# One transfer for the tail rows of the Q and K weights, all gate and up loads on one queue, and new orders for five engines

## The chip, the cores and the metric

The kernel runs on one core of a Trainium2 chip. The metric is the time of one execution in device microseconds; a profiled execution also gives the span, from the first to the last instruction of the program. Five engines work side by side: TensorE (PE in the profile; its weight loads are PEld), VectorE (DVE), ScalarE (ACT), GpSimd (POOL) and SyncE (SP). SP only issues transfers here. ACT issues some, between its activations.

## The reference

The computation is one transformer block on 2048 tokens of width 448: layer norm, linear attention with 16 heads of 28, a residual, a second layer norm, a gated Gelu MLP of width 1792, and a residual.

```python
def _A_ref(x, wqkv, wo):                      # x: layer norm of the input
    qkv = (x @ wqkv) ...                      # split into q, k, v by head
    phi = lambda t: jnp.where(t > 0, t + 1, jnp.exp(t)) + 1e-6
    pq, pk = phi(q), phi(k)
    kv = jnp.einsum("bhsd,bhse->bhde", pk, v)
    z = jnp.einsum("bhsd->bhd", pk)
    num = jnp.einsum("bhqd,bhde->bhqe", pq, kv)
    den = jnp.einsum("bhqd,bhd->bhq", pq, z)[..., None] + 1e-6
    return (num / den) ... @ wo

def _B_ref(x, w_gate, w_up, w_down):
    return (gelu(x @ w_gate) * (x @ w_up)) @ w_down

h = x + _A_ref(_layernorm(x), wqkv, wo)
h2 = h + _B_ref(_layernorm(h), w_gate, w_up, w_down)
```

Inputs and outputs are bf16; sums are kept in fp32.

## The kernel before

**Tiles.** The 2048 tokens are 16 tiles of 128. The width 448 is taken as three blocks of 128 rows and a tail of 64, so the weights of Q, K and V lie in four blocks of partitions; the fourth holds 64 rows of weights and 64 rows of zeros.

**First stage, per tile t.** DVE takes the statistics of the row (`bnst1_t`, L414, and `bnag1_t`, L415). ACT makes the inverse deviation with a logarithm and an exponential (`ln1_t`, `rstd1_t`, L421 and L423). Tiles 0 to 3 are normalized by DVE (`normD_t`, L436), transposed by PE (`tr0_t`, `tr1_t`, L444) and copied out in two halves, by ACT (`evxA_t`, L449) and DVE (`evxD_t`, L451). Tiles 4 to 15 are normalized by POOL (`negm1_t`, L418, `normP_t`, L454) and transposed by a transfer on SP's queue (`xT_t`, L456). Then PE projects (L470): step `k_t` or `q_t`, four matmuls of 448 columns, one for each block of rows, the fourth with the tail rows. ACT takes the exponential of K (`ek_t`, L481), DVE clips and adds (`ck_t`, L482, `pk_t`, L483), and PE sums the products of pk with the normalized rows over all tiles (`pt4_t`, from tile 10 on `pt1_t` and `pt3_t`, L489). For Q, ACT makes `eq_t` and `rq_t` (L497, L498). The projections take turns on four banks of PSUM, so each waits until the one four places earlier (in the order in which the program makes them) has been read.

**Middle.** The sums become, with the V weights, the key-value matrices (`kv`, L528), and with the output weights the matrices `w2` (L548). Two copies by transfer (`dws0`, `dws1`, written to `pt_sb`) swap the halves of `w2`. The denominators and scaled queries are made in pairs of tiles p (`cqP_p`, L583, `aqP_p`, L584, POOL's `t1p_t`, L586, `drP_p`, L587, ACT's `deP_p`, L589, `rdP_p`, L590, `pnP_p`, L591). They are transposed by a transfer (`oT_p`, L606), and PE makes the attention output in two steps (`outA_p`, `outB_p`, L628 and L629). DVE adds the residual (`hr_t`, L634) and takes the statistics of the second layer norm; POOL makes its power and negated mean (`vpe2`, `pow2`, `negm2`, L426, L427, L418) and normalizes (`nhP_t`, L663), DVE repeats the row once (`wrap_t`, L665), and SP's queue transposes (`hT_t`, L666).

**Last stage.** The MLP works on chunks of 2, 2, 4, 4 and 4 tiles. A step `gu2_v` or `gu4_v` (L727 gate, L729 up) is a set of matmuls with 64 rows: the gate weights and their rows lie on partitions 0 to 63, the up weights on 64 to 127, and a gate and an up matmul run side by side. In 14 steps of the first two chunks (7 each) and 14 of each later chunk the hidden width is covered. ACT takes the Gelu in two halves (`ge0_v`, `ge1_v`, L747), DVE multiplies with the up part (`hm0_v`, `hm1_v`, L749). The gate results take turns on two banks, the up results on two others, so step v needs the products of step v - 2. The down projection is done for pairs of tiles in two parts (`downA_p`, `downB_p`, L697), DVE adds the residual (`fo448_t`, L703), and SP stores the tile (`do_t`, L704; L683 and L684 for the last two tiles).

**What sets the order.** The program records 866 tasks, each with its engine and the buffers that it reads and writes; semaphores follow from these. The order on each engine is written out by hand as a list of task numbers (`ORDERS`), one list for each engine, and nothing moves at run time: an engine that waits for one task holds all tasks behind it in its list. `HOLD` only says which of several waits of a task is placed first. A transfer is issued by the engine whose list it is in, and each of SP and ACT has one queue of transfers; SP's is q1 in the profile, ACT's q10.

**Loads.** x comes in pieces on both queues. `dw0` and `dw1` are the first 384 rows of the K and Q weights, `dw0_t` and `dw1_t` their last 64 rows (the tails), all in `wqk_sb`: K's columns in the second half, Q's in the first. `dwg0` and `dwg1` are the gate weights (first 768 columns, then the rest), `dwu0` and `dwu1` the up weights. Every transfer of these is recorded by one helper, so that all have the line L347.

The loads around the change, before:

```python
dma_w1("act", wqk_sb, D, 2 * D, b_wk, "dw0_t")
tx1 = dma_w1("act", wqk_sb, 0, D, b_wq, "dw1_t")
...
dma("sp", wgu_sb[A_, :, cs], B_w_gate[:, cs]..., [b_wg[i]], "dwg%d" % i, after=xts[-1:])
dma("act", wgu_sb[B_, :, cs], B_w_up[:, cs]..., [b_wu[i]], "dwu%d" % i, after=eks[13:14])
```

Of the kernel before, what the change touches and what calls it, by code (L numbers as in the profile page):

```python
# [12 lines left out]


ORDERS = (
# [34 lines left out]
)  # L50
HOLD = {
# [3 lines left out]
}  # L55


# [173 lines left out]
def bass_sequential_preLN__linear_attn_block__glu_gated_geglu__prompt_kernel(  # L231
    nc, A_x, A_wqkv, A_wo, B_x, B_w_gate, B_w_up, B_w_down, out
):
    S, D, FF, H, DH = 2048, 448, 1792, 16, 28
# [16 lines left out]
    with es:  # L251
# [8 lines left out]
        wqk_sb = sb("wqk_sb", [128, 4, 2 * D], BF16)  # L260
# [45 lines left out]
        def bufs(name, n):  # L306
            return [_Buf("%s%d" % (name, i)) for i in range(n)]
# [4 lines left out]
        b_ones2 = _Buf("ones2")  # L312
        b_wq, b_wk, b_wv = bufs("wq", 2), bufs("wk", 2), bufs("wv", 2)
        b_wpad = bufs("wpad", 2)
        b_wo, b_wg, b_wu, b_wd = _Buf("wo"), bufs("wg", 2), bufs("wu", 2), _Buf("wd")
        b_ident, b_ones, b_mones, b_mtmp, b_mask, b_eps, b_mhalf, b_powtmp = (
            _Buf(n) for n in ("ident", "ones", "mones", "mtmp", "mask", "eps", "mhalf", "powtmp"))
# [28 lines left out]
        def dma(q, out_ap, in_ap, w, name, r=(), after=()):  # L346
            t_ = G.add(q, lambda e: e.dma_start(out_ap, in_ap), r=r, w=w, name=name, kind="dma", after=list(after) + last[q])  # L347
            last[q] = [t_]
            return t_
# [7 lines left out]
        def dma_w1(q, dst, c0, c1, b, name):  # L357
            return dma(q, dst[A_, 3, c0 % (2 * D):c0 % (2 * D) + c1 - c0], A_wqkv[384:448, c0:c1], [b[1]], name)
# [8 lines left out]
        dma_x("act", 1, 2)  # L367
        dma_x("sp", 2, 4)
        dma_w3("act", wqk_sb, D, 2 * D, b_wk, "dw0")
        dma_w1("act", wqk_sb, D, 2 * D, b_wk, "dw0_t")  # L370
        tx1 = dma_w1("act", wqk_sb, 0, D, b_wq, "dw1_t")
        dma_w3("sp", wqk_sb, 0, D, b_wq, "dw1")
        dma_x("sp", 4, 8)
        dma_x("sp", 8, 12)
# [84 lines left out]
        eks = []  # L459
# [11 lines left out]
            return ins  # L471

        def proj_reads(t, b):
            return [(b_xnT[t][0], 0), (b_xnT[t][1], 2), (b[0], 0), (b[1], 3), (b_wpad[0], 3)]

        def k_tile(t):
            bk = slot()
# [31 lines left out]
        for i in range(2):  # L509
            cs = slice(0, FC) if i == 0 else slice(FC, FF)  # L510
            dma("sp", wgu_sb[A_, :, cs], B_w_gate[:, cs].rearrange("(k p) n -> p k n", p=64), [b_wg[i]], "dwg%d" % i, after=xts[-1:])
            dma("act", wgu_sb[B_, :, cs], B_w_up[:, cs].rearrange("(k p) n -> p k n", p=64), [b_wu[i]], "dwu%d" % i, after=eks[13:14])


        op("act", lambda e: e.activation(zbc[B_, :], ps[B_, BK_PT[3], 0:D], AF.Identity), [b_ps[BK_PT[3]]], [b_z[1]], "z1")
# [303 lines left out]
```

## Time and profile before

| | us |
|---|---|
| median of 3 runs | 191.06 |
| lowest and highest | 191.03 and 191.11 |
| the profiled execution, its own time | 191.73 |
| its span, first to last instruction | 190.0 |
| PE busy in it | 184.9 |
| DVE busy | 127.8 |
| ACT busy | 76.6 |
| POOL busy | 51.6 |

The granted TensorE clock is 1.00 throughout. The profile stretches the execution a little: its own time is 0.67 us over the median. In a timeline row the first number is the start in us from the span's start, the second the duration of the row (a row can hold several equal instructions, "x8"), and what stands in brackets is the idle time before it and what ended that. The ends of matmuls are modelled, so two steps of PE are best compared from start to start. In the table of transfers the last number is the time from issue to landing. In the chain of waits each row names what the work that ended last was waiting for.

### The profile page before, as it was taken

How to read it: one execution, taken by the hardware profiler on the slowest of the kernel's cores; microseconds unless marked ns; L12 is line 12 of the kernel's file. 1: busy time of each engine (PE TensorE's matmuls, PEld its weight loads, DVE VectorE, ACT ScalarE, POOL GpSimd, SP SyncE). 2: the span in 40 equal slices, each digit the busy share in tenths (PEclk: the TensorE clock that was granted, in tenths of full speed). 3: DMA queues.
4: the chain of work that ended last, by engine and by line, in shares of the span. 5: the costliest groups of instructions: out<-in, count | busy, mean ns of one | idle time of the engine just before them, and what ended most of it. 6: DMA issues, size and time to landing. Idle time of an engine off the chain costs nothing.

```text
span 190.0 us, 4461 instructions
## 1 busy us (share of the span) xinstructions
PE 184.9 (97%) x1813; PEld 114.9 (60%) x1813; DVE 127.8 (67%) x328; ACT 76.6 (40%) x220; POOL 51.6 (27%) x91
## 2 busy tenths in 40 slices
PE   7899999999999999989999999999999999999994
PEld 7554555555689898855666666555544555555643
DVE  3998869999999995868976933592474234335232
ACT  3688843699963221334331421222244122224100
POOL 6066740514416569003484000019000000000000
PEclk9999999999999999999999999999999999999999
DMA  6995448999394432940020691000590000200004
GB/s 175 373 229 88 86 92 176 210 217 198 70 314 90 85 52 48 105 95 28 0 52 0 117 136 40 0 5 0 121 146 4 3 0 0 76 0 0 3 15 155
DMA packets 35076, 17.11 MB, mean 90 GB/s; under 512 B 26864, under 2 KB 33648, under 8 KB 35056
## 3 DMA queue, kind: packets, MB, share of 16 engines
q1 hardware_dynamic: 33424, 14.65, 37.6%
q10 hardware_dynamic: 1632, 2.18, 5.2%
q8 instruction: 14, 0.23, 0.5%
q14 instruction: 6, 0.05, 0.1%
HBM read 8.26 MB, written 1.84 MB: 53 GB/s over the span
## 4 chain that ended last, share of the span: by engine, by line
PE 78%; DVE 9%; DMA 8%; POOL 2%; SPq 1%; issue 1%; ACT 0%
PE ps L729 29%; PE ps L697 16%; PE ps L470 10%; PE ps L727 9%; PE ps L489 5%; DMA x_sb<-in_A_x_dram 3%; PE ps L679 3%; DMA hnT<-hn 2%; DMA xnT<-xnn 2%; PE ps L628 2%; DVE st L414 2%; POOL hn L663 2%; DVE hh L749 2%; PE ps L629 1%; DVE x_sb L634 1%; DVE pqn L591 1%
## 5 line engine op out<-in xcount | busy, mean ns | idle before, releaser
L727 PE MATMUL ps<-hnT,wgu_sb 64*128 64x512 bf16 (+1 forms) x490 | 89.0, 333 | 0.6 <-DMA hnT<-hn 0.6
L729 PE MATMUL ps<-hnT,wgu_sb 64*128 64x512 bf16 (+1 forms) x490 | 89.0, 333 | 0.0
L747 ACT ACTIVATE gl<-ps 128x256 bf16<-128x256 f32 x112 | 36.8, 381 | 85.0 <-PE ps L727 84.8
L749 DVE TENSOR_TENSOR hh<-ps,gl 128x256 bf16<-128x256 f32 x112 | 42.5, 415 | 36.3 <-ACT gl L747 35.7
L729 PEld LDWEIGHTS ps<-hnT,wgu_sb 64*128 64x128 bf16 x490 | 45.0, 94 | 26.5 <-DVE hh L749 3.0
L727 PEld LDWEIGHTS ps<-hnT,wgu_sb 64*128 64x128 bf16 x490 | 45.2, 94 | 6.0 <-ACT gl L747 0.8
L697 PE MATMUL ps<-wd_sb,hh 64*128 64x448 bf16 x392 | 41.5, 349 | 0.0
L697 PEld LDWEIGHTS ps<-wd_sb,hh 64*128 64x128 bf16 x392 | 24.3, 94 | 13.3 <-issue 0.2
L470 PE MATMUL ps<-wqk_sb,xnT 128*128 128x448 bf16 x128 | 27.3, 353 | 0.7 <-DMA wqk_sb<-in_A_wqkv_dram 0.6
L414 DVE BATCH_NORM_STATS2 st<-x_sb 128x6 f32<-128x448 bf16 x32 | 19.3, 613 | 2.2 <-DMA x_sb<-in_A_x_dram 2.2
L586 POOL TENSOR_TENSOR t<-pq,zbc 128x448 f32<-128x448 bf16 x12 | 13.0, 1104 | 28.4 <-DVE pq L584 28.4
L470 PEld LDWEIGHTS ps<-wqk_sb,xnT 128*128 128x128 bf16 x128 | 12.2, 98 | 12.1 <-DMA wqk_sb<-in_A_wqkv_dram 1.2
L703 DVE TENSOR_TENSOR x_sb<-ps,x_sb 128x448 bf16<-128x448 f32 x14 | 8.6, 617 | 8.9 <-PE ps L697 8.9
L489 PE MATMUL ps<-pk,xnn 128*128 128x448 bf16 x64 | 14.1, 352 | 0.0
L628 PE MATMUL ps<-w,pqnT 64*128 64x448 bf16 x49 | 11.5, 349 | 0.1
L426 POOL TENSOR_SCALAR ln<-mv 128x2 f32<-128x2 f32 x7 | 2.3, 330 | 32.3 <-DVE mv L415 32.0
L481 ACT ACTIVATE e<-ps 128x448 bf16<-128x448 f32 x16 | 8.7, 541 | 6.0 <-PE ps L470 6.0
L663 POOL TENSOR_SCALAR hn<-x_sb,nm,rs 128x448 bf16<-128x448 bf16 x14 | 10.6, 765 | 0.1
L629 PE MATMUL ps<-pt_sb,pqnT 64*128 64x448 bf16 x42 | 10.2, 349 | 0.0
L489 PEld LDWEIGHTS ps<-pk,xnn 128*128 128x128 bf16 x64 | 6.2, 98 | 6.0 <-DVE pk L483 0.8
L634 DVE TENSOR_TENSOR x_sb<-ps,x_sb 128x448 bf16<-128x448 f32 x16 | 9.6, 612 | 0.3 <-PE ps L629 0.3
L483 DVE SCALAR_TENSOR_TENSOR pk<-ps,e 128x448 bf16<-128x448 f32 x16 | 9.6, 611 | 0.1
(83 smaller groups left out, 159.2 us busy)
## 6 DMA issues: line engine op xcount, KB each, us to landing
out_dram<-x_sb SPq DMA_DIRECT2D x15, 112.0 KB, 1.8
wd_sb<-in_B_w_down_dram SPq DMA_DIRECT2D x1, 1568.0 KB, 7.6
x_sb<-in_A_x_dram SPq DMA_DIRECT2D x3, 448.0 KB, 6.6
wgu_sb<-in_B_w_gate_dram SPq DMA_DIRECT2D x1, 896.0 KB, 9.6
wgu_sb<-in_B_w_up_dram ACTq DMA_DIRECT2D x1, 896.0 KB, 12.8
wgu_sb<-in_B_w_gate_dram SPq DMA_DIRECT2D x1, 672.0 KB, 5.9
wgu_sb<-in_B_w_up_dram ACTq DMA_DIRECT2D x1, 672.0 KB, 10.4
wo_sb<-in_A_wo_dram SPq DMA_DIRECT2D x1, 392.0 KB, 8.1
```

The costliest lines, as they stand in the source:

```text
L414: op("dve", lambda e: e.bn_stats(st[:, t, :], src_ap), [b_src], [b_st[t]], "bnst%s_%d" % (tag, t))
L470: ins = e.matmul(ps[:, bk, 0:D], xnT[:, t, k, :], wqk_sb[:, k, c0:c0 + D], start=(k == 0), stop=(k == 3))
L489: ins = e.matmul(ps[:, BK_PT[c], 0:D], xnn[:, t % XN_R, c * 128:(c + 1) * 128], pk[:, ip, :], start=(t == 0), stop=(t == T - 1))
L586: op("pool", lambda e, n=n: e.tensor_tensor(t1[:, n, :], pq[:, a + n, :], zbc[:, :], ALU.mult), [b_pq[a + n]] + b_z, [b_t1[n]], "t1p_%d" % ...
L628: e.matmul(ps[:, BK_OUT[0], 0:D], pqnT[ra, i2, sg // 2, :], w2[ra, sg // 2, :], start=(sg == 0), stop=(sg == 5))
L629: ins = e.matmul(ps[:, BK_OUT[1], 0:D], pqnT[rb, i2, 3 + (sg + 1) // 2, :], (w2 if sg == 6 else w2s)[rb, sg // 2, :], start=(sg == 0), sto ...
L663: op("pool", lambda e, t=t, sh=sh: e.tensor_scalar(hn[:, sh, 0:D], x_sb[:, t, :], nm2[:, t:t + 1], rs2[:, t:t + 1], ALU.add, ALU.mult), [b ...
L697: ins = e.matmul(ps[:, BK_O[n], 0:D], hh[rows, j, sl[n]], wd_sb[rows, j, :], start=(half == 0 and j == 0), stop=(half == 1 and j == NJ - 1))
L727: first = e.matmul(psG[:, jj * N:(jj + 1) * N], wgu_sb[A_, k, j * 128:(j + 1) * 128], hnT[A_, ka_, c0:c0 + N], start=(k == 0), stop=(k == ...
L729: ins = e.matmul(psU[:, jj * N:(jj + 1) * N], wgu_sb[B_, k, j * 128:(j + 1) * 128], hnT[B_, kb_, c0:c0 + N], start=(k == 0), stop=(k == NK ...
L747: G.add("act", lambda e, gi=gi, cs_=cs_, psG=psG: e.activation(gl[:, gi, cs_], psG[:, cs_], AF.Gelu_apprx_tanh), r=[b_ps[BK_G[i]]], w=[b_g ...
L749: op("dve", lambda e, dst=dst, srcU=srcU, srcL=srcL: e.tensor_tensor(dst, srcU, srcL, ALU.mult), [b_ps[BK_U[i]], b_glh], [b_ar[j_][t % HR] ...
```

## The change

Three things are changed at once.

1. The two transfers of the last 64 rows, `dw0_t` (K) and `dw1_t` (Q), become one transfer `dw0_t` of 64 rows by 896 columns on ACT's queue. All projections, K and Q, now wait for the one buffer `b_wt` before their fourth matmul. There are 865 tasks instead of 866.
2. The up loads `dwu0` and `dwu1` move from ACT's list to SP's. SP issues `dwg0 dwu0 dwg1 dwu1` in a row behind the last transpose of x, and the swap copies `dws0 dws1` and the transpose `oT_1` follow.
3. The lists of all five engines are new (every number in them also shifts by one), and so is `HOLD`.

```diff
-        dma_w1("act", wqk_sb, D, 2 * D, b_wk, "dw0_t")
-        tx1 = dma_w1("act", wqk_sb, 0, D, b_wq, "dw1_t")
+        tx1 = dma("act", wqk_sb[A_, 3, :], A_wqkv[384:448, 0:2 * D], [b_wt], "dw0_t")
...
-            return [(b_xnT[t][0], 0), (b_xnT[t][1], 2), (b[0], 0), (b[1], 3), (b_wpad[0], 3)]
+            return [(b_xnT[t][0], 0), (b_xnT[t][1], 2), (b[0], 0), (b_wt, 3), (b_wpad[0], 3)]
...
-            dma("act", wgu_sb[B_, :, cs], B_w_up[:, cs].rearrange("(k p) n -> p k n", p=64), [b_wu[i]], "dwu%d" % i, after=eks[13:14])
+            dma("sp", wgu_sb[B_, :, cs], B_w_up[:, cs].rearrange("(k p) n -> p k n", p=64), [b_wu[i]], "dwu%d" % i, after=xts[-1:])
```

The lists, by the names of the tasks, where the prediction speaks of them ("-" before, "+" after):

```diff
 PE, start
-tr0_0 tr1_0 tr1_1 tr0_1 k_0 q_0 tr1_2 tr0_2 tr0_3 tr1_3 k_1 k_2 k_3 pt4_0 pt4_1 q_1 q_2 pt4_2 k_4 q_3 pt4_3 k_5
+tr0_0 tr1_0 tr0_1 tr1_1 k_0 tr0_2 tr1_2 k_1 q_0 tr0_3 tr1_3 k_2 k_3 pt4_0 q_1 pt4_1 pt4_2 q_2 k_4 pt4_3 k_5 q_3
 PE, middle
-pt3_13 q_4 pt3_14 pt3_15 q_5 q_6 kv q_7 q_10 w2_2 w2_1 w2_3 w2_0 tro_1 q_9 tro_0 q_8 out1_1 out1_0 q_11 q_12 q_13 q_15 q_14 trh_1
+pt3_13 pt3_14 pt3_15 q_5 q_4 kv q_7 q_8 w2_2 w2_0 w2_1 q_9 w2_3 tro_1 tro_0 q_6 out1_1 out1_0 q_10 q_11 q_13 q_12 q_14 q_15 trh_1
 PE, first two chunks of the MLP
-outA_3 gu2_6 outB_3 downA_0 gu2_7 gu2_8 downB_0 gu2_9 outA_4 gu2_10 outB_4 gu2_11 gu2_12 gu2_13 gu4_14 gu4_15 outA_5
+outA_3 gu2_6 outB_3 downA_0 gu2_8 gu2_7 downB_0 gu2_9 gu2_10 outA_4 gu2_11 outB_4 gu2_12 gu2_13 gu4_14 downA_1 gu4_15 outA_5
 DVE, start
-normD_1 bnag1_2 evxD_0 bnst1_3 bnag1_3 evxD_1 normD_2 normD_3 bnst1_4 ck_0 bnag1_4 evxD_2 pk_0 evxD_3 bnst1_5
+normD_1 bnag1_2 bnst1_3 evxD_0 bnag1_3 normD_2 evxD_1 normD_3 evxD_2 bnst1_4 ck_0 bnag1_4 bnst1_5 pk_0 bnag1_5 evxD_3
 DVE, from pair 3's pqn to the products of step 7
-pnP_3 hm0_2 cqP_5 hm1_2 hm0_3 hm1_3 cqP_4 hr_4 wrap_2 hr_5 aqP_4 wrap_3 ... drP_4 bnag2_5 aqP_5 bnag2_4 rdP_4 hm1_6 hm0_6 hr_7 pnP_4 hr_6 bnst2_6 bnst2_7 drP_5 bnag2_7 hm1_8 bnag2_6 hm0_7 rdP_5 hm1_7
+pnP_3 cqP_4 bnag2_2 bnag2_3 hm1_2 hm0_2 cqP_7 hr_4 hm1_3 hm0_3 hr_5 wrap_3 hm0_4 hm1_4 bnst2_4 aqP_7 wrap_2 aqP_4 ... cqP_5 bnst2_6 bnst2_7 drP_4 bnag2_7 bnag2_6 wrap_4 aqP_5 rdP_4 wrap_5 pnP_4 hm1_8 hm0_7 hm0_8 hm1_7
 ACT, start and around step 8
-rstd1_3 ek_0 evxA_2 evxA_3 ln1_4 rstd1_4 ek_1 ... ge1_6 ge1_8 ge1_7 deP_5 ge0_8 ge0_7
+rstd1_3 ek_0 evxA_2 ek_1 ln1_4 rstd1_4 evxA_3 ... ge1_6 ge0_6 ge0_8 deP_4 ge1_7 ge0_7 ge1_8
 POOL, second layer norm of tiles 4 to 7
-t1p_10 vpe2_4 pow2_4 t1p_11 vpe2_6 negm2_6 pow2_6 negm2_4 nhP_6 nhP_5 nhP_4 nhP_7
+t1p_8 t1p_9 vpe2_4 pow2_4 negm2_4 nhP_4 nhP_5 vpe2_6 pow2_6 negm2_6 t1p_10 nhP_7 nhP_6 t1p_11
 SP
-xT_15 dwg0 dwg1 dws0 dws1 oT_1 oT_2 dwd oT_3 hT_2 hT_3 oT_4 hT_6 hT_5 hT_7 hT_4 oT_5 do_1 oT_6 oT_7 hT_9
+xT_15 dwg0 dwu0 dwg1 dwu1 dws0 dws1 oT_1 oT_2 dwd oT_3 hT_3 hT_2 hT_4 oT_4 hT_5 hT_7 hT_6 oT_5 oT_6 hT_9 ... oT_7
 SP, the last stores
-do_13 do_7 do_11 do_10 do_12 do_15 do_14 do_15
+do_12 do_3 do_6 do_2 do_13 do_10 do_14 do_7 do_15
```

In the changed kernel's profile the lines are one to two lower than before (L470 becomes L468, L666 becomes L664).

More of the change, by code (lines that the diff above doesn't have):

```diff
@@ L15 @@
 ORDERS = (
[34 rows of a table removed]
[33 rows of a table added]
 )
 HOLD = {
[3 rows of a table removed]
+    65: (35,), 140: (139,), 164: (163,), 213: (212,), 215: (214,), 322: (301,), 325: (323,), 430: (339,), 703:
+    (563,), 734: (733,), 780: (671,), 838: (835,), 848: (845,),
 }
@@ L314, in bass_sequential_preLN__linear_attn_block__glu_gated_geglu__prompt_kernel @@
         b_wpad = bufs("wpad", 2)
+        b_wt = _Buf("wt")
         b_wo, b_wg, b_wu, b_wd = _Buf("wo"), bufs("wg", 2), bufs("wu", 2), _Buf("wd")
```

70 rows, old and new, of tables (HOLD, ORDERS) are left out of this document.

## The prediction

> **What bounds the kernel now.** The page comes first: its busy shares, the DVE slices and the chain that ended last.
>
> ```profile
> span 190.0 us, 4461 instructions
> PE 184.9 (97%) x1813; PEld 114.9 (60%) x1813; DVE 127.8 (67%) x328; ACT 76.6 (40%) x220; POOL 51.6 (27%) x91
> ...
> DVE  3998869999999995868976933592474234335232
> ...
> PE 78%; DVE 9%; DMA 8%; POOL 2%; SPq 1%; issue 1%; ACT 0%
> ```
>
> TensorE (PE) is busy for 97% of the span, and nothing here takes a matmul away (the weights, tiles and matmul counts stay). So the change can only move PE's waits. VectorE (DVE) is full, or nearly, between slices 2 and 16 (4.75 us each: 5 to 76 us): there a DVE order decides. The profiled execution took 191.73 us, which is its span and 1.73 us around it. The median of the three runs, 191.06, is 0.67 us less. I work out the change of the span and take it from the median.
>
> I then followed the timeline of PE to see where the start of a step comes later than the step before it needs.
>
> ```profile
> 6.33 1.49 PE L470 MATMUL ps<-wqk_sb,xnT 128*128 128x448 bf16 x7
> 8.39 0.36 PE L470 MATMUL ps<-wqk_sb,xnT 128*128 128x448 bf16 x1 [0.57 <-DMA wqk_sb<-in_A_wqkv_dram]
> ...
> 12.82 1.68 PE L470 MATMUL ps<-wqk_sb,xnT 128*128 128x448 bf16 x8
> 14.33 0.92 PE L489 MATMUL ps<-pk,xnn 128*128 128x448 bf16 x4
> 15.37 0.93 PE L470 MATMUL ps<-wqk_sb,xnT 128*128 128x448 bf16 x4
> ```
>
> Eight matmuls take 14.33 - 12.82 = 1.51 us from start to start, so one step of four (K, Q or pt of a tile) takes 0.755. Seven from 6.33 end their slots at 7.65, but the eighth (the last of Q0, which needs the tail rows of the Q weights) starts at 8.39: **0.74 us lost**. After 14.33 the next step could start at 15.09; it starts at 15.37: **0.28 lost**. What ended these two waits, and one more, stands in the chain of waits:
>
> ```profile
> 10.93 4.40 DMA xnT<-xnn
> ...
> 77.67 4.61 DMA hnT<-hn
> ```
>
> and, at the third place, in PE's timeline:
>
> ```profile
> 80.00 0.27 PE L727 MATMUL ps<-hnT,wgu_sb 64*128 64x256 bf16 x1
> 80.11 0.27 PE L727 MATMUL ps<-hnT,wgu_sb 64*128 64x256 bf16 x1
> ...
> 82.37 0.37 PE L727 MATMUL ps<-hnT,wgu_sb 64*128 64x512 bf16 x1 [0.57 <-DMA hnT<-hn]
> ```
>
> K4 waits for the transpose of tile 4. The gate and up step 13 has 14 pairs at 0.11 us, 1.53 in all, so step 14 could start at 81.53; it waits for the transposes of tiles 4 to 7 until 82.37: **0.84 lost**. These three, 1.86 us, are nearly all that an order can give back; elsewhere PE's steps follow each other without a gap.
>
> **Part 1: one transfer for the tail rows.** The two transfers of 64 rows become one of the same bytes.
>
> ```profile
> 1.26 1.67 ACTq L347 DMA_DIRECT2D wqk_sb<-in_A_wqkv_dram  x3
> ...
> 6.80 0.58 PEld L470 LDWEIGHTS ps<-wqk_sb,xnT 128*128 128x128 bf16 x4 [0.18 <-DMA wqk_sb<-in_A_wqkv_dram]
> ```
>
> The K tail came just before 6.80, the Q tail just before 8.39, 1.6 us apart. One transfer lands between these two (below 6.80 only if its half-sized predecessor's rows were not the limit, which I exclude; it is issued at the same place). Its 64 rows are as many as each half had, only twice as long, so I take 7.2, nearer to the 6.80; the range keeps both ends. One issue of 1.67 / 3 = 0.56 us leaves ScalarE's (ACT's) queue; that brings the table load forward and nothing behind it, as the first activation waits for DVE's statistics.
>
> But now K0, not only Q0, needs all of it, and the new DVE order adds two waits. It puts the statistics of tile 3 ahead of the copy of tile 0's transposed half, and the statistics of tile 5 ahead of pk of tile 0:
>
> ```profile
> 6.05 0.26 DVE L451 COPY xnT<-ps 128x256 bf16<-128x256 bf16 x1
> ...
> 6.23 0.61 DVE L414 BATCH_NORM_STATS2 st<-x_sb 128x6 f32<-128x448 bf16 x1
> ...
> 9.01 0.66 ACT L449 ACTIVATE xnT<-ps 128x256 bf16<-128x256 bf16 x2 [0.96 <-PE ps L444]
> ```
>
> The copy ends about 0.53 later (0.61 less the overlap of neighbours, 0.08): at 6.84 for 6.31. K0's third matmul was due at 6.33 + 2 x 0.19 = 6.71 and starts at 6.89, +0.18; its fourth is due at 7.08 and waits to 7.2, +0.12. K3, which takes the bank that pk of tile 0 frees, waits another 0.3 (one such statistics step, less what PE was late). So 0.74 of wait becomes 0.6, and PE is ready for K4 at 15.09 - 0.14 = 14.95. The transpose of tile 4 can be issued about 0.4 earlier (an estimate): ScalarE has that tile's variance behind these two copies (0.66), which came late since PE was late; now one of them stands behind the variance, and the other is no longer late. At the same 4.40 us it lands at 10.93 - 0.4 + 4.4 = 14.93. K4 starts at 14.95 instead of 15.37: **0.4 us gained**. Ends: 0.75 gained (tail at 6.8 and no wait for pk), 0.45 lost (tail at 8.35, below).
>
> **Part 2: the K, Q and pt steps to 50 us.** The statistics of tiles 11 to 15 move ahead of pk of tiles 4 to 6. DVE had two extra of them (0.61 each) before pk4 and one before pk6, against idle time in the trace of about the same. The transposes of x come out of SP's queue sooner, so PE does not wait there. Cost taken 0.1, between 0 and 0.6 (one statistics step not covered). One Q step moves from ahead of the kv step to behind the first outputs: as many PE steps in all, and DVE gets 0.755 more before the second layer norm is needed. I take 0.
>
> **Part 3: the up loads on SP's queue.**
>
> ```profile
> L347 ACTq DMA_DIRECT2D wgu_sb<-in_B_w_up_dram x2: 622/638/653, 31.5 to 33.6; - x2
> ...
> 28.37 1.33 SPq L347 DMA_DIRECT2D wgu_sb<-in_B_w_gate_dram  x2
> 41.76 1.17 SPq L347 DMA_DIRECT2D pt_sb<-w  x2
> ...
> wgu_sb<-in_B_w_gate_dram SPq DMA_DIRECT2D x1, 896.0 KB, 9.6
> wgu_sb<-in_B_w_up_dram ACTq DMA_DIRECT2D x1, 896.0 KB, 12.8
> wgu_sb<-in_B_w_gate_dram SPq DMA_DIRECT2D x1, 672.0 KB, 5.9
> wgu_sb<-in_B_w_up_dram ACTq DMA_DIRECT2D x1, 672.0 KB, 10.4
> pt_sb<-w SPq DMA_DIRECT2D x2, 168.0 KB, 5.7
> ```
>
> The gates were issued at 28.4 and 29.0 and landed at 34.3 and 38.7; the ups at 31.5 and 33.6, landing at 41.9 and 46.4. Each lands 3 to 4.5 us after the one before: they already ran one after another, and the swap copies (pt_sb<-w, issued at 41.8, landing about 47.5) already came behind the last up load. Two more issues of 0.64 us fall into SP's idle stretch between 29.7 and 41.8, which hides them; uncovered they would cost 1.3. The swap copies and the transpose of pair 1 are queued behind. ACT loses two issues in idle time. I take 0.
>
> The Trainium skill ("DMA: Bandwidth & Descriptors", section "Queues, rings and completion order") says that each DMA engine takes turns between the queue rows that have work. By that rule the swap copies shared the engines with the up loads before and lose this now; this trace disagrees, since they landed behind the last up load although their own queue was empty.
>
> **Part 4: POOL, SP and DVE from 50 to 82 us.** Here the largest wait goes.
>
> ```profile
> 66.98 1.51 POOL L427 TENSOR_TENSOR rs<-ln,mhalf 128x2 f32<-128x2 f32 x1
> ...
> 71.69 0.71 POOL L427 TENSOR_TENSOR rs<-ln,mhalf 128x2 f32<-128x2 f32 x1
> 72.37 0.22 POOL L418 TENSOR_SCALAR nm<-mv 128x2 f32<-128x2 f32 x1
> 72.58 3.17 POOL L663 TENSOR_SCALAR hn<-x_sb,nm,rs 128x448 bf16<-128x448 bf16 x4
> ...
> 73.65 5.76 SPq L666 DMA_TRANSPOSE hnT<-hn  x4
> ```
>
> Tiles 4 and 5 had their power at 68.49, but their negated mean stood behind tiles 6 and 7's, at 72.37. All four normalizations came in one block, and all four transposes in one burst; the last took 4.61 us to land. The new POOL order normalizes 4 and 5 right after their power; SP sends tile 4 ahead of the transpose oT_4, and 5, 7 and 6 behind it. So the burst at the end has two transposes (5.76 / 4 = 1.44 each) less, 2.9 us. I give one of them back for the product of pair 5 that POOL now does ahead of tiles 6 and 7. The last one is issued at 77.67 - 1.44 = 76.2 and lands, even at 4.61, at 80.8: before 81.5. **0.84 gained**, 0 at worst.
>
> What it costs: the minimum and addition of pair 7 (L583, L584) come forward into this stretch, while the sum and reciprocal of pair 5 (L587, L590) go behind, so the DVE work ahead of step 7's products stays about level. Yet step 9 needs step 7's last product, and in the new order (8 before 7 on PE) that is the last of four products behind three Gelus:
>
> ```profile
> L747 ACT ACTIVATE gl<-ps 128x256 bf16<-128x256 f32 x112 | 36.8, 381 | 85.0 <-PE ps L727 84.8
> L749 DVE TENSOR_TENSOR hh<-ps,gl 128x256 bf16<-128x256 f32 x112 | 42.5, 415 | 36.3 <-ACT gl L747 35.7
> ```
>
> Step 7's matmuls end 2.65 us (the 14 pairs of downB_0 at 0.19) before step 9 starts. Into these go some 0.2 until the first Gelu, three Gelus (0.38 each, less the 0.1 that neighbours overlap: 0.94) and four products (0.42, less 0.08: 1.42), 2.56 in all, if DVE comes free of pair 4's pqn in time. Cost taken 0.1, between 0 and the rival's price.
>
> **Part 5: the end.** PE's order of the last eleven steps stays.
>
> ```profile
> 184.19 2.30 SPq L704 DMA_DIRECT2D out_dram<-x_sb  x5
> 186.53 1.84 SPq L684 DMA_DIRECT2D out_dram<-x_sb  x3
> ```
>
> Seven outputs stand in a row ahead of the last one before; now eight do (tile 7's store comes behind tile 14's). At 2.30 / 5 = 0.46 each they end just when the last result is ready, but one more store of 112 KB is in flight: 0.1 lost, between 0 and 0.4.
>
> **Sum:** 0.4 - 0.1 + 0.84 - 0.1 - 0.1 = 0.94 us off. 191.06 - 0.94 = **190.1 us**.
>
> **The rivals.** *The single tail is late* (8.35, as the Q tail): K0 waits there instead of Q0, one more step comes behind it, and K4 starts at 15.84, 0.47 later than before. The time: 191.06 + 0.47 + 0.3 - 0.84 = 191.0. Against it: the same number of rows as the first half. Chance 0.06.
>
> *The transposes stay late.* If the last one takes its place behind oT_4 and a slow landing, the 0.84 stays: 190.9. Against it: two fewer in the burst. Chance 0.06.
>
> *Slower: DVE and POOL hold each other up between 50 and 76 us.* The same instruction takes different times there:
>
> ```profile
> 57.50 0.39 DVE L583 TENSOR_SCALAR eq<-eq 128x896 bf16<-128x896 bf16 x1
> 58.57 1.54 POOL L663 TENSOR_SCALAR hn<-x_sb,nm,rs 128x448 bf16<-128x448 bf16 x2
> 58.92 0.61 DVE L583 TENSOR_SCALAR eq<-eq 128x896 bf16<-128x896 bf16 x1
> ...
> 66.85 1.07 DVE L591 TENSOR_TENSOR pqn<-pq,rd 128x896 bf16<-128x896 bf16 x1
> ```
>
> The slow one (+0.22) lies beside POOL's two normalizations, and POOL's power took 1.51 instead of 0.71 beside the 1.07 of pqn. The new order packs more such pairs together. Two powers at +0.8 and three minima at +0.22 make 2.3 us in one chain (power, normalization, wrap, pqn, step 7's product), against a slack of 0.1 there: 190.1 + 2.0 = 192.1. It decides once the product comes over 1.3 us late. For it: DVE has no idle time there. Against: most of the chain's rows already hold such times. Chance 0.23.
>
> The Trainium skill ("SBUF — State Buffer", section "SBUF: two separate sides") calls the port that both engines share an exclusive lock: the one that starts second blocks fully. The 1.51 beside the 1.07 agrees; this rival is that rule at work.
>
> *Loads on one queue are slower than in turns.* The transpose of pair 1 then holds outA_1; it takes 2 us more of loading to be felt: about 192. The rows above show no gap between loads of one queue. Chance 0.03.
>
> **How the numbers follow.** The forecast has 0.62, the slower two 0.26, the two near 191 0.12. A change under 0.2% (0.38 us) is about what a measurement here cannot tell: 190.68 to 191.44 is "same". Faster 0.62, same 0.12, slower 0.26. The range runs from 189.2 (part 1 at its best, no small costs: 1.59, with 0.3 for the terms taken at 0) to 191.9, short of the slower rival's own 192.1, of which about half lies beyond.
>
> **What would show it.** Right: no wait on wqk_sb over 0.4 us; K4 near 14.95; no PE wait on hnT at step 14; up loads landing one behind the other by about 46. Wrong: K0's last matmul at 8.3; an idle PE at step 9 with DVE hh as its releaser; outA_1 released by the transpose later than 49.2.

## The result, and the profile after

The changed kernel takes 191.12 us (median of 22 executions, 190.37 to 191.67); the kernel before, timed beside it, 191.56 (22 executions, 191.03 to 192.86). The ratio is 0.9971, 95% interval 0.9957 to 0.9985: 0.55 us faster, where 0.94 was forecast. Over all timings the means are 191.53 for before (the 175 executions timed beside the other kernels) and 191.03 for the change (46).

Two things stand out. The three executions from which the forecast counted down (191.03 to 191.11) lie at the low end of the kernel before, 0.47 under its mean. And only about half of the gain came.

The page after: the busy shares hardly move. In the chain that ended last PE's share rises from 78% to 93%, and POOL drops out.

```profile
span 188.9 us, 4454 instructions
PE 184.3 (98%) x1813; PEld 108.4 (57%) x1813; DVE 127.8 (68%) x328; ACT 76.4 (40%) x220; POOL 50.0 (26%) x91
...
DVE  4999859999899998786796762562744343345232
...
PE 93%; DMA 3%; DVE 2%; ACTq 0%; issue 0%
```

TensorE's timeline at the places that the prediction named: K0 and K4, the kv step, and gate and up steps 13 and 14.

```profile
6.32 0.92 PE L468 MATMUL ps<-wqk_sb,xnT 128*128 128x448 bf16 x3
7.46 0.36 PE L468 MATMUL ps<-wqk_sb,xnT 128*128 128x448 bf16 x1 [0.23 <-DMA wqk_sb<-in_A_wqkv_dram]
...
14.16 1.68 PE L468 MATMUL ps<-wqk_sb,xnT 128*128 128x448 bf16 x8
...
34.59 1.68 PE L468 MATMUL ps<-wqk_sb,xnT 128*128 128x448 bf16 x8
36.32 1.03 PE L526 MATMUL ps<-pt_sb,wv_sb 128*112 128x112 bf16 x16
...
79.64 0.27 PE L725 MATMUL ps<-hnT,wgu_sb 64*128 64x256 bf16 x1
...
81.17 0.38 PE L725 MATMUL ps<-hnT,wgu_sb 64*128 64x512 bf16 x1
```

- K0's last matmul starts at 7.46, when the joined tail is in (1.74 + 5.68 = 7.42, below). Without any wait it would start at 6.32 + 3 x 0.19 = 6.89, so K0 loses 0.57 us: 0.18 at its third matmul, as forecast, and 0.4 at the tail, where the prediction had 0.12.
- The row at 14.16 holds Q2 and K4: K4 starts at 14.16 + 0.755 = 14.92 (forecast 14.95).
- Step 13 takes 81.17 - 79.64 = 1.53 us, its own work. Step 14 does not wait: the 0.84 are gone.
- New: two Q steps start at 34.59 and end their slots at 36.10, but kv starts at 36.32. **0.22 us lost** where before nothing was.

The chain of waits names what kv waited for, beside the joined tail:

```profile
1.74 5.68 DMA wqk_sb<-in_A_wqkv_dram
33.09 0.62 DVE pt_sb L515
35.74 0.54 DVE pt_sb L520
```

The last row is DVE's copy of quarter 2 of P. P is the sum of the products of pk with the rows, kept in four quarters. In the groups of transfers the loads of gate and up follow each other, and the last up load lands near 46, as forecast:

```profile
wgu_sb<-in_B_w_gate_dram SPq DMA_DIRECT2D x1, 896.0 KB, 12.2
wgu_sb<-in_B_w_up_dram SPq DMA_DIRECT2D x1, 896.0 KB, 16.5
wgu_sb<-in_B_w_gate_dram SPq DMA_DIRECT2D x1, 672.0 KB, 6.1
wgu_sb<-in_B_w_up_dram SPq DMA_DIRECT2D x1, 672.0 KB, 8.6
...
pt_sb<-w SPq DMA_DIRECT2D x2, 168.0 KB, 5.9
```

The columns are the size of a transfer and the time from issue to landing. With issues at 27.66, 28.37, 29.04 and 29.71 they land at 33.8, 37.0, 41.2 and 46.3.

### The profile page after: what moved, and what is told of

The parts are those of the page before. It is cut to its first block, busy times and chain, and to the rows that moved or that the text cites. A ratio compares the mean times of both kernels' runs of the same rounds, so it can differ in the third digit from the quotient of the medians.

```text
span 188.9 us, 4454 instructions
## 1 busy us (share of the span) xinstructions
PE 184.3 (98%) x1813; PEld 108.4 (57%) x1813; DVE 127.8 (68%) x328; ACT 76.4 (40%) x220; POOL 50.0 (26%) x91
## 4 chain that ended last, share of the span: by engine, by line
PE 93%; DMA 3%; DVE 2%; ACTq 0%; issue 0%
PE ps L727 38%; PE ps L695 19%; PE ps L468 12%; PE ps L725 9%; PE ps L487 6%; DMA wqk_sb<-in_A_wqkv_dram 3%; PE ps L677 3%; PE ps L626 3%; PE ps L627 2%; PE ps L616 1%; PE ps L546 1%; PE ps L526 1%; ACTq L346 0%; PE ps L653 0%; DVE den L571 0%; DVE pt_sb L515 0%
## 5 line engine op out<-in xcount | busy, mean ns | idle before, releaser
L695 PEld LDWEIGHTS ps<-wd_sb,hh 64*128 64x128 bf16 x392 | 22.7, 94 | 14.9 <-issue 0.2
L468 PE MATMUL ps<-wqk_sb,xnT 128*128 128x448 bf16 x128 | 27.5, 353 | 0.2 <-DMA wqk_sb<-in_A_wqkv_dram 0.2
L468 PEld LDWEIGHTS ps<-wqk_sb,xnT 128*128 128x128 bf16 x128 | 12.2, 98 | 11.7 <-DMA wqk_sb<-in_A_wqkv_dram 0.5
L584 POOL TENSOR_TENSOR t<-pq,zbc 128x448 f32<-128x448 bf16 x12 | 12.3, 1042 | 23.7 <-DVE pq L582 22.0
L661 POOL TENSOR_SCALAR hn<-x_sb,nm,rs 128x448 bf16<-128x448 bf16 x14 | 9.9, 719 | 0.4
```

Of the source, the lines that this page charges most:

```text
L468: ins = e.matmul(ps[:, bk, 0:D], xnT[:, t, k, :], wqk_sb[:, k, c0:c0 + D], start=(k == 0), stop=(k == 3))
L584: op("pool", lambda e, n=n: e.tensor_tensor(t1[:, n, :], pq[:, a + n, :], zbc[:, :], ALU.mult), [b_pq[a + n]] + b_z, [b_t1[n]], "t1p_%d" % ...
L661: op("pool", lambda e, t=t, sh=sh: e.tensor_scalar(hn[:, sh, 0:D], x_sb[:, t, :], nm2[:, t:t + 1], rs2[:, t:t + 1], ALU.add, ALU.mult), [b ...
L695: ins = e.matmul(ps[:, BK_O[n], 0:D], hh[rows, j, sl[n]], wd_sb[rows, j, :], start=(half == 0 and j == 0), stop=(half == 1 and j == NJ - 1))
```

## The experiments

"Early" is the part up to about 50 us (to the first output product), "late" the part behind. A kernel of half and half takes the order of each engine from one kernel for all instructions begun by the cut, and the other kernel's order for the rest.

**1. The halves, each alone, and both kernels again.**

```
late_only:   early orders and all loads of before | late orders of the change
early_only:  early orders and all loads of the change | late orders of before
```

> The kernel before, unchanged, timed against itself: the ratio says what these runs can tell apart, and its profile is a second execution of the same program. Theory A (the first profile of before showed waits that most executions don't have): here K4 waits less than 0.28 us for the transpose of tile 4, or step 14 less than 0.84 us for the transposes of tiles 4 to 7, and the two together come to 0.6 us or less. Theory B (those waits are in every execution, and the new order loses something elsewhere): the two waits are again 1.0 to 1.2 us together. Ratio 1.000 within 0.0015 by both.

> The changed kernel, unchanged, a second execution. Theory A: the same places as in its first profile (K4 near 14.9, no PE wait for hnT at step 14), a ratio near 0.997. Theory B: a wait of 0.3 us or more at some PE step that the first profile did not have, ratio also near 0.997.

> Parts 1, 2 and 3 alone: the new loads and the new orders up to about 50 us, the orders of before behind that. Forecast by the prediction's terms: 0.4 - 0.1 = 0.3 us off (ratio 0.9984). Theory A: 0.1 to 0.3 off, of which the shorter wait for the tail weights (0.74 to 0.6) is the steady part. Theory B with the loss in this half: 0 or up to 0.3 slower.

> Parts 4 and 5 alone: the loads and orders of before up to about 50 us, the new orders behind that. Forecast by the prediction's terms: 0.84 - 0.1 - 0.1 = 0.64 us off (ratio 0.9967). Theory A: 0.2 to 0.4 off, since step 14 of before waits less in most executions. Theory B with the loss in this half: 0 or less. PE does not wait for hnT at step 14 by any of them.

Measured, as ratio to before: before_again 1.0004 (0.9983 to 1.0024), after_again 0.9972 (0.9957 to 0.9988), early_only **1.0034** (1.0014 to 1.0054), late_only **0.9965** (0.9949 to 0.9980). The late half alone gives all that the whole change gives, and somewhat more; the early half alone is slower. Theory B holds, with its loss in the early half.

But the waits that the prediction priced do differ between executions, as theory A has it. Steps 13 and 14 and K4 in the second profile of before:

```profile
14.78 1.49 PE L470 MATMUL ps<-wqk_sb,xnT 128*128 128x448 bf16 x7
...
79.39 0.27 PE L727 MATMUL ps<-hnT,wgu_sb 64*128 64x256 bf16 x1
...
81.39 0.37 PE L727 MATMUL ps<-hnT,wgu_sb 64*128 64x512 bf16 x1 [0.20 <-issue]
```

Here step 14 comes 2.00 us behind step 13 and loses 0.47 (0.84 in the first profile, 0.99 in early_only; the last transpose lands 0.1 us before step 14 in all three), and K4 starts at 14.78 without a wait (15.37 in the first). In every trace with the late orders of the change the distance is 1.53. Their times lie closer together too: late_only 190.42 to 191.29, before, timed beside it, 190.90 to 192.68.

One thing goes together with the wait at K4 in all twenty traces. Early in each a packet of 16 KB moves on the profile's instruction queue (q8), 0.9 to 1.5 us long, at 13.0 to 16.0 us (19.7 in tail_first, below). The slowest of the first four transposes of x (3.5 to 4.4 us to landing, against 2.4 to 2.5 in quiet stretches) is always one that is in flight then. Where the packet starts at 13.0 to 13.4 us (the first profile of before, late_only, best_again), that is the transpose of tile 4, and it lands at 15.2 to 15.6, just before K4. In the other seventeen it is a later tile's, and K4 does not wait for its own. No run moves that packet, so this is seen and not tested; but it makes the 0.28 us at K4 a wait that most executions in these traces don't have.

In early_only the earlier start does not last: its gate and up step 0 starts at 50.36 (before: 50.76), its step 14 at 82.34 (82.37). So what PE gains early it waits for again at step 14, if that still waits for its transposes. Why early_only is slower by 0.6 us, and not merely level, its one trace does not show: that execution took 191.76, 0.42 under the kernel's mean of 192.18.

**2. The parts of the early half.**

```
late_and_tail: late_only, tail loads dw0_t and dw1_t -> one load
up_on_act:     the change, dwu0, dwu1: SyncE's queue -> ScalarE's
evp_first:     the change, DVE:  t1d_0 dr_0 evpD_2 rd_0 dr_1 -> t1d_0 evpD_2 dr_0 dr_1 rd_0
head_dve:      the change, DVE:  bnst1_3 evxD_0 -> evxD_0 bnst1_3
                                 bnst1_5 pk_0   -> pk_0 bnst1_5
late_tail_sp:  late_and_tail, dwu0, dwu1: ScalarE's queue -> SyncE's
tail_first:    late_and_tail, ScalarE:  dw0 dw0_t -> dw0_t dw0
```

> The orders of late_only (before's up to about 50 us, the new ones behind), with the two tail loads joined into one, as the changed kernel has it. Theory H (the joined tail is a small gain and the new head order spends it): K0's last matmul near 7.4, Q0 without a wait, so 0.35 us less waiting than in late_only and 0.2 to 0.35 us off its time, 190.5 to 190.6. Theory T (the joined tail itself costs): the tail lands behind 7.8, or K4 starts at 15.3 or later all the same, as its transpose does; no time is gained on late_only.

> The changed kernel with the two up loads back on ScalarE's queue. The prediction takes 0 for this part: same time as the changed kernel within 0.15 us, loads landing near 34, 38.7, 41.9 and 46.3 as before. Rival: the move to SyncE's queue costs 0.2 to 0.4 us (two more issues there, or ScalarE's), then this kernel is that much faster than the changed one.

> late_and_tail with the two up loads on SyncE's queue, in all other orders unchanged. By the prediction's part 3: no change (190.6 to 190.9), ups landing one behind the other up to about 46. Rival, from up_on_act (0.2 us under the changed kernel): 0.2 us slower than late_and_tail.

> The changed kernel with one DVE step moved: the PSUM copy of quarter 2 of P (evpD_2) ahead of the product for the denominator of tile 0 (dr_0). Theory: the kv step waits 0.25 us for this copy in all three executions that have the new early order (kv 0.22 and 0.12 lost) and in none of those with the old one, since one Q step less stands ahead of it; with the copy first kv starts without a wait at 36.1 (in an execution whose K4 starts at 14.9) and 0.2 to 0.3 us come off the time of the changed kernel (ratio to before 0.9955 to 0.9965). Rival: what waits next (the steps that take kv's result, or rd_0 on DVE) eats it, no change.

> The changed kernel with two statistics steps of DVE put back behind what PE waits for: those of tile 3 behind the copy of tile 0's transposed half, those of tile 5 behind pk of tile 0. Theory H: K0's third matmul comes at 6.71 (not 6.89), K3 never waits for pk of tile 0 (0.45 in one of three executions), and 0.1 to 0.4 us come off. Rival: the tail weights (7.4) and the transpose of tile 4 hide both, no change, K4 near 14.9 to 15.4 as now.

> late_and_tail with the joined tail issued ahead of the large load of K weights on ScalarE's queue. In late_and_tail K0's last matmul waits 0.35 us for the tail (7.4). If the tail lands by 7.0 and the large load by 6.3, the wait goes and up to 0.35 us come off (190.4 to 190.7, faster than both kernels). Rival: the large load then lands behind 6.5 and K0 starts later by as much, or the transpose of tile 4 keeps K4 at 14.8: no gain, or 0.2 to 0.5 us lost.

| kernel | ratio to before (95%) | mean us |
|---|---|---|
| late_and_tail | 0.9960 (0.9942 to 0.9978) | 190.77 |
| up_on_act | 0.9965 (0.9950 to 0.9980) | 190.84 |
| late_tail_sp | 0.9955 (0.9935 to 0.9974) | 190.75 |
| evp_first | 0.9982 (0.9969 to 0.9995) | 191.00 |
| head_dve | 0.9978 (0.9964 to 0.9991) | 191.02 |
| tail_first | 1.0179 (1.0142 to 1.0215) | 195.13 |

- *The joined tail* (late_and_tail): 0.39 us are lost at K0 and none at Q0 (late_only: 0.17 and 0.60), and K4 came at 14.81. But in the copies of this head K4 starts at 15.00 (late_tail_sp) and 15.62 (best_again, below); in late_only at 15.25, 15.42 and 15.30. The time, 190.77 against 190.75 over 35 executions of late_only, shows no gain.
- *The up loads*: 0.2 us for ScalarE's queue in one pair (190.84 against 191.03), 0.02 the other way in the other (190.77 against 190.75). The prediction's 0 stands within what these runs can tell.
- *evp_first*: kv starts without a wait, and the time is that of the change (191.00 against 191.03). Its rival held: the trace loses 0.16 and 0.19 at two steps behind kv instead, and 0.26 at K13, whose transpose is on the chain:

```profile
23.68 3.57 DMA xnT<-xnn
```

- *head_dve*: no change, so its rival held.
- *tail_first* is a miss that shows how much the place of a load counts. The tail lands at 5.2, but the large K load, issued 0.57 us later than else, lands at 10.05 instead of 5.35, and K0 waits for it. The load's group in tail_first, then in late_and_tail, and the timeline of tail_first:

```profile
wqk_sb<-in_A_wqkv_dram ACTq DMA_DIRECT2D x1, 336.0 KB, 8.2
```

```profile
wqk_sb<-in_A_wqkv_dram ACTq DMA_DIRECT2D x1, 336.0 KB, 4.1
```

```profile
10.19 3.15 PE L481 MATMUL ps<-wqk_sb,xnT 128*128 128x448 bf16 x8 [3.84 <-DMA wqk_sb<-in_A_wqkv_dram]
```

**3. Cuts at K4: inconclusive.**

```
head_new:  orders of the change up to K4 | before to 50 us | the change
mid_new:   before (with the joined tail) up to K4 | the change
```

> late_and_tail with the changed kernel's orders up to K4 (15 us), the orders of before from there to about 50 us, the new ones behind. Theory H (the head is even: what the new DVE order adds in waits, it gives back by an earlier transpose of tile 4): K4 between 14.8 and 15.4, the time of late_and_tail within 0.15 us (190.6 to 190.9). Theory H2 (the new head costs): 0.2 to 0.4 us slower than late_and_tail, K4 at 15.0 or later in the trace.

> The changed kernel with the orders of before (and the joined tail) up to K4, the new orders from there. Theory M (the stretch from 15 to 50 us is where the new order loses): kv waits again 0.2 to 0.3 us, and one K or Q step before it 0.2 to 0.27 in some executions; 0.2 to 0.4 us slower than late_and_tail. Theory H2: the time of late_and_tail.

Ratios 1.0011 (0.9997 to 1.0025) and 1.0046 (1.0030 to 1.0062): both slower than either parent, since the orders do not fit at the seam. In head_new PE waits for ScalarE just behind K4, in mid_new for DVE a little later:

```profile
16.75 0.93 PE L479 MATMUL ps<-wqk_sb,xnT 128*128 128x448 bf16 x4 [1.08 <-ACT pq L507]
```

```profile
19.21 0.93 PE L480 MATMUL ps<-wqk_sb,xnT 128*128 128x448 bf16 x4 [1.23 <-DVE pk L493]
```

These stalls are in neither parent, so the two kernels tell nothing of the change.

**4. Three waits of the new order mended together, with controls.**

```
mended, PE:  k_6 pt4_4 -> pt4_4 k_6
             k_13 pt4_9 -> pt4_9 k_13
             kv q_7 -> q_7 kv
```

> The changed kernel with three PE steps moved by one place each: K6 behind pt of tile 4, K13 behind pt of tile 9 (each gives the tile's transpose 0.75 us more to land), and one Q step (tile 7) back ahead of kv. Theory M (these three margins are what the early half loses): no wait at K6, K13 and kv, 0.25 to 0.4 us off the changed kernel, the time of late_only (190.7 to 190.85). Rival W (each wait only hides the next one, as with evp_first, where the steps behind kv waited instead): a wait of 0.2 us or more at the steps that take kv's result or pk's, and the time of the changed kernel (191.0 to 191.2).

> The changed kernel, unchanged, for a comparison on the same chip and a third profile: 191.0 to 191.2; K6 and K13 with under 0.4 us between the landing of their transpose and their start.

> late_only again on this chip: 190.7 to 190.95, that is 0.2 to 0.4 us under the changed kernel (the early half's cost). If it is within 0.1 us of the changed kernel, the early half costs nothing and the difference seen before was scatter.

> late_tail_sp again (orders of before to 50 us with the joined tail and the up loads on SyncE's queue, the new orders behind that): 190.5 to 190.8, faster than the changed kernel by 0.3 to 0.5 us and at or under late_only, by up to 0.26 us for the joined tail.

Ratios: mended 1.0028 (1.0011 to 1.0046), after_3 0.9971 (0.9951 to 0.9990), late_only_2 0.9958 (0.9939 to 0.9976), best_again 0.9975 (0.9956 to 0.9994). Moving three steps by one place made the kernel 1 us slower than the change (192.01 against 190.94). The waits moved on. One of them, pt of tile 7 for its pk:

```profile
24.58 0.93 PE L497 MATMUL ps<-pk,xnn 128*128 128x448 bf16 x4 [0.24 <-DVE pk L491]
```

Four places in its trace lose 0.41, 0.33, 0.29 and 0.14. Rival W held and was too mild.

**5. The Q step at kv by itself.**

```
kv_early:  late_only, PE:  q_5 q_6 kv -> q_5 kv q_6
```

> late_only with one move on PE: the Q step of tile 6 goes from ahead of kv to behind it, as the changed kernel has one Q step less there. By the prediction (0 for this move, since PE has as many steps in all): the time of late_only. Theory M: kv is due 0.75 us earlier, before DVE has copied quarter 2 of P; it waits 0.3 to 0.5 us, the steps behind it come that much later, and 0.25 to 0.5 us are lost against late_only (191.0 to 191.3).

> late_only again on this chip, for the comparison with kv_early: 190.7 to 190.9, kv without a wait.

late_only_3 0.9963 (0.9950 to 0.9977), kv_early **1.0023** (1.0013 to 1.0034): 1.09 us lost for one move (191.79 against 190.70). First late_only_3's timeline, then kv_early's:

```profile
35.73 1.68 PE L481 MATMUL ps<-wqk_sb,xnT 128*128 128x448 bf16 x8
37.25 0.99 PE L539 MATMUL ps<-pt_sb,wv_sb 128*112 128x112 bf16 x16
38.07 1.68 PE L481 MATMUL ps<-wqk_sb,xnT 128*128 128x448 bf16 x8
39.58 1.49 PE L559 MATMUL ps<-wo_sb,hh 112*128 112x448 bf16 x7
```

```profile
35.41 0.92 PE L481 MATMUL ps<-wqk_sb,xnT 128*128 128x448 bf16 x4
36.64 1.03 PE L539 MATMUL ps<-pt_sb,wv_sb 128*112 128x112 bf16 x16 [0.31 <-ACT pt_sb L531]
37.51 1.68 PE L481 MATMUL ps<-wqk_sb,xnT 128*128 128x448 bf16 x8
39.50 0.93 PE L481 MATMUL ps<-wqk_sb,xnT 128*128 128x448 bf16 x4 [0.32 <-ACT eq L508]
40.27 1.49 PE L559 MATMUL ps<-wo_sb,hh 112*128 112x448 bf16 x7
```

In late_only_3 two Q steps stand behind the last pt step and cover the copies of P, and kv starts as the second ends. With one Q step, kv is due at 35.41 + 0.755 = 36.16 and starts at 36.64: 0.48 lost. The Q step now behind kv comes late for ScalarE's exponentials, and the third one waits another 0.48 for the bank that these free (due 37.51 + 1.51 = 39.02, starts 39.50). The two make 0.96 of the 1.09.

This is not quite the move that the change makes. The change takes a Q step (tile 4) out from between the last pt steps and puts one of tile 6 far behind kv, so that six Q steps instead of seven precede kv, but two still stand behind the last pt step. kv_early takes one of these two away, and its kv waits for ScalarE's copy, where the changed kernel's waits for DVE's.

## Why the prediction was right in one half and wrong in the other

**The late half (parts 4 and 5): right, and a little better.** Forecast 0.64 off; late_only is 0.78 off by the means (191.53 - 190.75) and 0.73 by its mean ratio (0.9965, 0.9958, 0.9963). The step 14 wait is gone in every trace: in the first profile after, the last transpose is issued at 75.30 and lands at 80.4 (forecast 76.2 and 80.8). Its 0.84 is within what three traces of the old late orders show (0.47, 0.84, 0.99). Part 4's small cost of 0.1 did not come: the way from step 0 to step 9 takes 21.70 us instead of 21.80, so step 9 does not wait. Part 5's came, and a little more: from step 14 to the end of the span there are 107.77 us instead of 107.61. Of these 0.16, 0.05 lie on PE (103.76 instead of 103.71 to the last step), and 0.1 in the last store (1.64 us to landing instead of 1.53).

**The slower rival did not come.** POOL's power took 1.51 beside pqn; POOL's timeline after has it at 0.92 and 0.79 us, and the normalizations in two blocks:

```profile
65.20 0.92 POOL L425 TENSOR_TENSOR rs<-ln,mhalf 128x2 f32<-128x2 f32 x1
...
66.54 1.42 POOL L661 TENSOR_SCALAR hn<-x_sb,nm,rs 128x448 bf16<-128x448 bf16 x2
...
69.14 0.79 POOL L425 TENSOR_TENSOR rs<-ln,mhalf 128x2 f32<-128x2 f32 x1
70.02 0.44 POOL L416 TENSOR_SCALAR nm<-mv 128x2 f32<-128x2 f32 x1
...
71.45 1.42 POOL L661 TENSOR_SCALAR hn<-x_sb,nm,rs 128x448 bf16<-128x448 bf16 x2
```

The second power meets DVE's pqn all the same, but starts ahead of it:

```profile
69.28 1.08 DVE L589 TENSOR_TENSOR pqn<-pq,rd 128x896 bf16<-128x896 bf16 x1
```

This pqn takes 1.08 us, and 1.09 where POOL does nothing beside it (79.21 us). By the Trainium skill's exclusive lock ("SBUF — State Buffer", section "SBUF: two separate sides") the one that starts second, here pqn, would have been blocked to the power's end at 69.93; this trace does not show that. The negated mean behind the power starts under pqn and takes 0.44 instead of 0.23 us. So the meeting cost about 0.3 us here, not 0.8; no run tests the rule itself.

**The early half (parts 1 and 2): wrong.** Forecast 0.3 off, and it costs. The change against late_only, timed beside each other: 191.06 against 190.84 and 190.94 against 190.73; over all 46 and 35 executions 0.28 ± 0.13 slower; by the mean ratios, 0.9971 against 0.9962, 0.18. Three steps failed:

- *Part 1, "0.4 us gained" at K4*: the largest term. The start in the first profile was hit (14.92 for 14.95), but by luck. K0 lost 0.57 us instead of 0.30, K3 nothing instead of 0.3, and the transpose of tile 4 landed at 13.45 (10.65 + 2.80) and not at 14.93, so that PE no longer waited for it. In the second profile K3 waits 0.44 for pk of tile 0, and K4 starts at 15.36. The wait that was to go belonged to the one execution that was read. With the old head K4 starts at 15.37, 14.78, 15.25, 15.42, 15.30 and 14.98 (before twice, late_only three times, kv_early), with that of the change at 14.92, 15.36, 14.84, 14.77, 15.05, 14.95 and 14.99 (after, after_again, after_3, early_only, up_on_act, evp_first, mended): 0.2 sooner on average, with about 0.6 us between executions of the same head.
- *Part 2, "One Q step moves from ahead of the kv step"*, taken at 0. Each trace that has this part of the new orders unchanged shows the same loss there: kv comes 2.30 us behind the last pt step (after, after_again, after_3, early_only, head_dve, mid_new; 2.31 in up_on_act) instead of 2.08 (before, before_again and all three of late_only). The reason given, "as many PE steps in all", counted PE's work and not what the moved step covered. The rows of DVE's copies of quarters 3 and 2 of P and of PE, first before, then after:

```profile
33.75 0.62 DVE L517 CAST pt_sb<-ps 64x448 bf16<-64x448 f32 x1
...
36.32 0.61 DVE L522 CAST pt_sb<-ps 128x448 bf16<-128x448 f32 x1
```

```profile
34.68 1.30 PE L489 MATMUL ps<-pk,xnn 128*128 128x448 bf16 x6
35.81 1.68 PE L470 MATMUL ps<-wqk_sb,xnT 128*128 128x448 bf16 x8
37.33 0.99 PE L528 MATMUL ps<-pt_sb,wv_sb 128*112 128x112 bf16 x16
```

```profile
33.09 0.62 DVE L515 CAST pt_sb<-ps 64x448 bf16<-64x448 f32 x1
...
35.65 0.61 DVE L520 CAST pt_sb<-ps 128x448 bf16<-128x448 f32 x1
```

Quarter 3 is summed first (pt1), and its copy starts a run of work on DVE that ends with the copy of quarter 2, 3.18 us later before (36.93) and 3.17 after (36.26). Between the last pt1 step and kv PE had three Q steps to cover that run, and has two now. So before, the copy was done 0.40 us ahead of kv (37.33); after, kv is due at 36.10, and the copy is not done.
- *Part 2, "The transposes of x come out of SP's queue sooner, so PE does not wait there".* Not for tiles 6 and 13. From landing to the start of their K step there are 0.34 and 0.08 us in the first profile of the change, 0.32 and 0.21 in the second, where the kernel before had 2.60 and 1.07. Tile 13's is even issued later (23.73 instead of 23.11), since it is now the tenth in SP's list and was the ninth. The three profiles of the change itself show no wait there, but of seven traces with the new early orders of PE three lose 0.2 to 0.27 at K6 or K13 (up_on_act, evp_first, head_dve).

**What the steps come to.** In the traces nearly everything behind K4 is fixed. From K4 to step 0 it takes 35.38 to 35.43 us with the old orders (nine traces) and 35.58 to 35.61 with the new ones (after, after_again, after_3, early_only): about 0.2 lost, the kv step. From step 0 to the end of the span it takes 138.42 to 138.45 in all seventeen traces with the late orders of the change. So the span of an execution without a trace gives an estimate of its K4, if these two stretches are the same there; a late transpose of tile 6 or 13 then counts as a later K4. Timed beside each other, the change and late_only come to 15.23 and 15.23 on average, and to 15.12 and 15.13 (each good to about 0.1). By this estimate the new head gains nothing that can be seen where 0.4 was forecast, and the loss at kv is about the whole of the 0.2 us by which the change is slower than late_only. (The profiled executions of the change start step 0 at 50.63 on average and those of late_only at 50.74, but they also took 190.86 and 190.94 on average, where the kernels' means are 191.03 and 190.75.)

What **stays open** is why the wait at kv can't be won back. Inside the new order, taking it away (evp_first, mended) gained nothing, as other waits came behind it or elsewhere.

**Part 3 (0) held** within about 0.2 us, in two pairs. The swap copies take 5.9 us to landing instead of 5.7, behind the up loads on one queue as on two. Turns between the queues, as the Trainium skill has them ("DMA: Bandwidth & Descriptors", section "Queues, rings and completion order"), are not seen in the first profile either: the second gate load landed 4.43 us behind the first (34.29 to 38.72) although an up load had been issued on the other queue at 31.48, and on the one queue after it lands 4.29 us behind the load ahead of it (36.95 to 41.24).

**The base.** Of the distance from 190.1 to 191.12 half is missing gain (0.94 less 0.44 by the two medians) and half the base: 191.06 against 191.56 beside the change. Three executions within 0.08 us of each other looked like a sharp median; the same kernel spreads over 2 us. That the profiled execution took 191.73 was a sign: its waits were probably longer than those of the three from which they were taken off. Counted from 191.73 the same sum gives 190.8.

**What beats both.** late_only, with 190.75 (35 executions), is 0.2 to 0.3 faster than the change and 0.7 to 0.8 faster than before. late_tail_sp, which adds the joined tail and the up loads on SyncE's queue, comes out about the same (190.75, and 190.99 as best_again).

## What to carry to other kernels

When a step moves on the busiest engine, ask what ran beneath it: a step that only fills time may be the cover of another engine's run of work, and its move costs whatever then sticks out, not zero. Price a wait that ends with a transfer from several traces, since such waits differ by half a microsecond between executions, and take the gain off the execution in which the waits were read, not off a faster one. And a tuned order is a whole: two orders joined at K4, or one wait mended, moved the wait on here; the seam at 50 us cost late_only nothing.

## What was not expected of the hardware

A load of 336 KB issued 0.57 us later on its queue, behind one of 112 KB, landed 4.7 us later (10.05 for 5.35), while x and the Q weights came in on the other queue. The transposes by transfer take 2.4 to 2.5 us from issue to landing in quiet stretches for x and 2.9 for the second layer norm, and up to 4.4 and 5.8. The same one differs between executions: tile 4's of x took 4.40 and 2.90 in the two profiles of before. A slow one among the first four of x goes together with a 16 KB packet on the instruction queue in every trace here.
